# One ring and one order for all transfers of a scale-and-add kernel, with a head block of 512 rows

## The chip, the cores and the metric

The kernel runs on one core of one Trainium2 chip. Times are device microseconds (us) of one execution; a quoted time is the median of several executions. The profile gives the span from the first to the last instruction, which is about 1.3 us shorter than the time.

## The reference, cut to what matters

```python
B, S, D = 1024, 16, 512        # bfloat16
x, y  = normal * 0.05          # (B, S, D): 16384 rows of 1 KiB each
gamma = 1e-4 * normal * 0.05   # (D)
return x + gamma * y
```

Two tensors of 16.78 MB are read and one is written: 50.33 MB for hardly any arithmetic. Because gamma is so small, a result that pairs the wrong rows of y with x can still pass the correctness test; one that misplaces x cannot.

## The kernel before

Each of the 128 partitions owns 128 consecutive rows. y is multiplied by gamma in place on VectorE (DVE), then x is added in place, in four pieces of 53, 11, 53 and 11 rows. x has a buffer of 64 rows only, so its later loads wait until the first add has freed their place. SP (SyncE) issues the loads on its ring, ACT (ScalarE) issues gamma and the stores on its own. In the lists, `('x', 64, 117, 0)` is rows 64 to 117 of every partition, loaded to buffer row 0.

```python
PIECES = [53, 11, 53, 11]
SP = [('y', 0, 4), ('y', 4, 64), ('x', 0, 64, 0), ('y', 64, 128), ('x', 64, 117, 0), ('x', 117, 128, 64)]
ACT = [('g',), ('s', 0, 64), ('s', 64, 128)]
RELEASE = ('x', 64, 117, 0)
...
    xv = xf.rearrange("(p n) d -> p n d", p=P)       # 128 KiB from partition to partition
...
            if kind == "s" and not went:              # the first store waits for the hold
                _take(s_go, 1, eng)
                went = True
            if need > known:                          # and for the adds of its rows
                eng.wait_ge(s_add, need)
                known = need
...
    _take(s_load[RELEASE], 16, nc.tensor)             # x 64-117 has landed:
    nc.tensor.sem_inc(s_go, 1)                        # stores may be issued
    nc.tensor.sem_inc(s_rel, 1)                       # and VectorE may add
```

I call the last part *the hold*: no store is issued before x 64-117 has landed.

Of the kernel before, what the change touches and what calls it, by code (L numbers as in the profile page):

```python
# [3 lines left out]


PIECES = [53, 11, 53, 11]



SP = [('y', 0, 4), ('y', 4, 64), ('x', 0, 64, 0), ('y', 64, 128), ('x', 64, 117, 0), ('x', 117, 128, 64)]  # L10
ACT = [('g',), ('s', 0, 64), ('s', 64, 128)]

EARLY = (2, 0)


RELEASE = ('x', 64, 117, 0)

DVE = [('m', 0), ('m', 1), ('a', 0), ('a', 1), ('m', 2), ('m', 3), ('a', 2), ('a', 3)]
MULT, ADD = mybir.AluOpType.mult, mybir.AluOpType.add


def _take(sem, n, eng):


    return eng.wait_ge(sem, n).then_inc(sem, -n)  # L25


def kernel(
    tc: tile.TileContext,
    x: bass.AP,  # L30
    y: bass.AP,
    gamma: bass.AP,
    out: bass.AP,
):



    nc = tc.nc
    P = nc.NUM_PARTITIONS
    tc.close()  # L40
    tc.compile()  # L41

    xf = x.flatten_outer_dims()
    yf = y.flatten_outer_dims()
    of = out.flatten_outer_dims()
    N, D = xf.shape
    rows = N // P
    n = len(PIECES)
    assert sum(PIECES) == rows
    starts = [sum(PIECES[:c]) for c in range(n + 1)]  # L50
    dt = xf.dtype
    xv = xf.rearrange("(p n) d -> p n d", p=P)
    yv = yf.rearrange("(p n) d -> p n d", p=P)
    ov = of.rearrange("(p n) d -> p n d", p=P)

    gamma_row = nc.alloc_sbuf_tensor("gamma_row", [1, D], dt).ap()
    ones_row = nc.alloc_sbuf_tensor("ones_row", [1, P], dt).ap()
    gamma_sb = nc.alloc_sbuf_tensor("gamma_sb", [P, D], dt).ap()
    y_sb = nc.alloc_sbuf_tensor("y_sb", [P, rows, D], dt).ap()
    x_loads = [w for w in SP + ACT if w[0] == "x"]  # L60
    y_loads = [w for w in SP + ACT if w[0] == "y"]
    stores = [w for w in SP + ACT if w[0] == "s"]
    for loads in (x_loads, y_loads, stores):
        assert sum(w[2] - w[1] for w in loads) == rows
    x_rows = max(w[3] + w[2] - w[1] for w in x_loads)
    x_sb = nc.alloc_sbuf_tensor("x_sb", [P, x_rows, D], dt).ap()
    gamma_ps = nc.alloc_psum_tensor("gamma_ps", [P, D], mybir.dt.float32).ap()

    sem = nc.alloc_semaphore
    s_gamma, s_ones, s_ps, s_dve = sem("s_gamma"), sem("s_ones"), sem("s_ps"), sem("s_dve")  # L70
    s_load = {w: sem("s_" + "_".join(map(str, w[:2]))) for w in x_loads + y_loads}
    s_add, s_go, s_rel, s_end, s_out = sem("s_add"), sem("s_go"), sem("s_rel"), sem("s_end"), sem("s_out")
    added = [a for kind, *a in DVE if kind == "a"]
    order = {a[0]: k for k, a in enumerate(added)}

    def meets(a, b, c, d):
        return a < d and c < b

    def pieces_of(a, b):
        return [c for c in range(n) if meets(starts[c], starts[c + 1], a, b)]  # L80

    def x_at(row):
        return next(w[3] + row - w[1] for w in x_loads if w[1] <= row < w[2])

    def frees(w):

        c = set()
        for v in x_loads[: x_loads.index(w)]:
            lo, hi = max(v[3], w[3]), min(v[3] + v[2] - v[1], w[3] + w[2] - w[1])
            if lo < hi:  # L90
                c |= set(pieces_of(v[1] + lo - v[3], v[1] + hi - v[3]))
        return sorted(c)

    early = []

    def ring(eng, what, n_early):

        known, went = 0, False
        for k, w in enumerate(what):
            kind = w[0]  # L100
            need = frees(w) if kind == "x" else pieces_of(w[1], w[2]) + list(w[3:]) if kind == "s" else []
            need = max((order[c] + 1 for c in need), default=0)
            if kind == "s" and not went:
                _take(s_go, 1, eng)
                went = True
            if need > known:
                eng.wait_ge(s_add, need)
                known = need
            if kind == "g":
                i = eng.dma_start(out=gamma_row, in_=gamma.unsqueeze(0)).then_inc(s_gamma, 16)  # L110
            elif kind == "x":
                to = x_sb[:, w[3] : w[3] + w[2] - w[1], :]
                i = eng.dma_start(out=to, in_=xv[:, w[1] : w[2], :]).then_inc(s_load[w], 16)
            elif kind == "y":
                r = slice(w[1], w[2])
                i = eng.dma_start(out=y_sb[:, r, :], in_=yv[:, r, :]).then_inc(s_load[w], 16)
            else:
                r = slice(w[1], w[2])
                i = eng.dma_start(out=ov[:, r, :], in_=y_sb[:, r, :]).then_inc(s_out, 16)
            if k < n_early:  # L120
                early.append(i.ins)

    ring(nc.sync, SP, EARLY[0])
    ring(nc.scalar, ACT, EARLY[1])


    nc.vector.memset(ones_row, 1.0).then_inc(s_ones, 1)  # L127
    _take(s_ones, 1, nc.tensor)
    _take(s_gamma, 16, nc.tensor)
    nc.tensor.matmul(gamma_ps, ones_row, gamma_row, start=True, stop=True).then_inc(s_ps, 1)  # L130
    _take(s_ps, 1, nc.vector)
    nc.vector.tensor_copy(out=gamma_sb, in_=gamma_ps).then_inc(s_dve, 1)  # L132
    _take(s_dve, 1, nc.vector)

    _take(s_load[RELEASE], 16, nc.tensor)
    nc.tensor.sem_inc(s_go, 1)
    nc.tensor.sem_inc(s_rel, 1)

    landed, open_mults = set(), 0

    def need(loads, c):
        for w in loads:
            if w not in landed and meets(starts[c], starts[c + 1], w[1], w[2]):
                if w == RELEASE:
                    _take(s_rel, 1, nc.vector)
                else:
                    _take(s_load[w], 16, nc.vector)
                landed.add(w)

    for kind, *args in DVE:  # L150
        c = args[0]
        yt = y_sb[:, starts[c] : starts[c + 1], :]
        if kind == "m":
            need(y_loads, c)
            g = gamma_sb[:, None, :].to_broadcast([P, PIECES[c], D])
            nc.vector.tensor_tensor(out=yt, in0=yt, in1=g, op=MULT).then_inc(s_dve, 1)  # L156
            open_mults += 1
        else:
            need(x_loads, c)
            if open_mults:  # L160
                _take(s_dve, open_mults, nc.vector)
                open_mults = 0
            at = x_at(starts[c])
            xt = x_sb[:, at : at + PIECES[c], :]
            nc.vector.tensor_tensor(out=yt, in0=xt, in1=yt, op=ADD).then_inc(s_add, 1)  # L165


    nc.scalar.sem_inc(s_end, 1)
    _take(s_end, 1, nc.sync)
    _take(s_add, n, nc.sync)  # L170
    _take(s_out, 16 * len(stores), nc.sync)

    main = nc.main_func.blocks[0].instructions
    names = {i.name for i in early}
    for b in nc.main_func.blocks[1:]:
        for i in [i for i in b.instructions if i.name in names]:
            b.instructions.remove(i)
    for k, i in enumerate(early):
        main.insert(1 + k, i)
# [30 lines left out]
```

## Time and profile before

| | before |
|---|---|
| time, median of 3 | 119.98 us (119.96 to 120.91) |
| span of the profile | 118.7 us |
| VectorE busy | 70.0 us (59%) |
| packets of both rings, share of 16 engines' span | 66.0% + 32.6% |

The lines of the page, the issue list and the timeline are in the prediction. One view is added here, the waits of SP's own queue: who waited for whom, us in total, times, longest us.

```profile
SPq L25 <- SPq L25: 62.0, 2, 39.3
SPq L113 <- DVE y_sb L165: 53.0, 1, 53.0
```

The second line is SP standing still before it issues x 64-117, until the first add is done. It costs nothing: x 64-117 is issued from 55.78 on, and the transfers issued earlier keep the engines busy until y 64-128 lands at 60.56. The first is its two waits at the program's end.

Some numbers below come from the trace's records of single DMA packets and of completions, which no printed view lists: a packet's start, bytes and duration, and the time at which each of the 16 engines completed a transfer. I say "packet records" where I use them.

### The profile page before, as it was taken

How to read it: one execution, taken by the hardware profiler on the slowest of the kernel's cores; microseconds unless marked ns; L12 is line 12 of the kernel's file. 1: busy time of each engine (PE TensorE's matmuls, PEld its weight loads, DVE VectorE, ACT ScalarE, POOL GpSimd, SP SyncE). 2: the span in 40 equal slices, each digit the busy share in tenths (PEclk: the TensorE clock that was granted, in tenths of full speed). 3: DMA queues.
4: the chain of work that ended last, by engine and by line, in shares of the span. 5: the costliest groups of instructions: out<-in, count | busy, mean ns of one | idle time of the engine just before them, and what ended most of it. 6: DMA issues, size and time to landing. Idle time of an engine off the chain costs nothing. (4 is left out here: it accounts for less than half of the span.)

```text
span 118.7 us, 80 instructions
## 1 busy us (share of the span) xinstructions
PE 0.6 (0%) x1; PEld 0.1 (0%) x1; DVE 70.0 (59%) x10; POOL 0.2 (0%) x4
## 2 busy tenths in 40 slices
PE   0001000000000000000000000000000000000000
PEld 0000000000000000000000000000000000000000
DVE  0002000599999299999759999999999910000000
POOL 0000000000000000000000000000000000000000
DMA  8977977998899888998896969498899889988891
GB/s 268 571 332 331 663 331 331 596 464 353 353 486 574 353 353 353 640 420 353 353 585 293 585 293 585 205 634 353 353 596 464 353 353 420 640 353 353 353 663 44
DMA packets 1154, 50.33 MB, mean 424 GB/s; under 512 B 129, under 2 KB 130, under 8 KB 258
## 3 DMA queue, kind: packets, MB, share of 16 engines
q1 hardware_dynamic: 864, 33.55, 66.0%
q10 hardware_dynamic: 290, 16.78, 32.6%
HBM read 33.56 MB, written 16.78 MB: 424 GB/s over the span
## 5 line engine op out<-in xcount | busy, mean ns | idle before, releaser
L156 DVE TENSOR_TENSOR y_sb<-y_sb,gamma_sb 128x27136 bf16<-128x27136 bf16 (+1 forms) x4 | 34.6, 8688 | 12.3 <-DVEq L25 12.3
L165 DVE TENSOR_TENSOR y_sb<-x_sb,y_sb 128x27136 bf16<-128x27136 bf16 (+1 forms) x4 | 34.6, 8689 | 2.3 <-DVEq L25 2.2
L132 DVE CAST gamma_sb<-gamma_ps 128x512 bf16<-128x512 f32 x1 | 0.7, 692 | 8.8 <-DVEq L25 8.8
L127 DVE MEMSET ones_row<- 1x128 bf16 x1 | 0.2, 165 | 2.0 <-PEq L41 2.0
L130 PE MATMUL gamma_ps<-gamma_row,ones_row 1*128 1x512 bf16 x1 | 0.6, 577 | 10.2 <-PEq L25 10.2
L130 PEld LDWEIGHTS gamma_ps<-gamma_row,ones_row 1*128 1x128 bf16 x1 | 0.1, 99 | 10.2 <-issue 10.2
L194 POOL MEMSET const-bfloat16-1.0<- 128x1 bf16 x1 | 0.1, 101 | 0.0
L194 POOL MEMSET const-uint8-127<- 128x1 uint8 x1 | 0.1, 101 | 0.0
L194 POOL MEMSET const-float32-0.0<- 128x1 f32 x1 | 0.1, 98 | 0.2 <-issue 0.2
L194 POOL MEMSET const-float32-1.0<- 128x1 f32 x1 | 0.1, 98 | 0.0
## 6 DMA issues: line engine op xcount, KB each, us to landing
y_sb<-in_y_dram SPq DMA_DIRECT2D x1, 7680.0 KB, 21.4
x_sb<-in_x_dram SPq DMA_DIRECT2D x1, 6784.0 KB, 20.8
x_sb<-in_x_dram SPq DMA_DIRECT2D x1, 1408.0 KB, 23.8
y_sb<-in_y_dram SPq DMA_DIRECT2D x1, 512.0 KB, 3.8
out_dram<-y_sb ACTq DMA_DIRECT2D x2, 22.8
x_sb<-in_x_dram SPq DMA_DIRECT2D x1, 39.3
gamma_row<-in_gamma_dram ACTq DMA_DIRECT2D x1, 1.0 KB
y_sb<-in_y_dram SPq DMA_DIRECT2D x1, 58.3
```

The source lines that it names most:

```text
L127: nc.vector.memset(ones_row, 1.0).then_inc(s_ones, 1)
L130: nc.tensor.matmul(gamma_ps, ones_row, gamma_row, start=True, stop=True).then_inc(s_ps, 1)
L132: nc.vector.tensor_copy(out=gamma_sb, in_=gamma_ps).then_inc(s_dve, 1)
L156: nc.vector.tensor_tensor(out=yt, in0=yt, in1=g, op=MULT).then_inc(s_dve, 1)
L165: nc.vector.tensor_tensor(out=yt, in0=xt, in1=yt, op=ADD).then_inc(s_add, 1)
L194: nc = _bacc.Bacc("TRN2", target_bir_lowering=False, num_devices=1)
```

## The change

The intent: put every transfer on one ring in the order in which it is wanted, so that no hold and no second ring are needed; and let the first, small loads read one contiguous block.

```diff
-SP = [('y', 0, 4), ('y', 4, 64), ('x', 0, 64, 0), ('y', 64, 128), ('x', 64, 117, 0), ('x', 117, 128, 64)]
-ACT = [('g',), ('s', 0, 64), ('s', 64, 128)]
-RELEASE = ('x', 64, 117, 0)
+HEAD = 4
+RING = [("y", 0, HEAD), ("y", HEAD, 64), ("x", 0, HEAD, 0), ("x", HEAD, 64, HEAD), ("y", 64, 128),
+        ("x", 64, 117, 0), ("x", 117, 128, 64),
+        ("s", 0, HEAD), ("s", HEAD, 64), ("s", 64, 128)]
...
-    xv = xf.rearrange("(p n) d -> p n d", p=P)      # and yv, ov
+    def rows_of(t, a, b):
+        head = t[: P * HEAD].rearrange("(p n) d -> p n d", p=P)
+        body = t[P * HEAD :].rearrange("(p n) d -> p n d", p=P)
+        return head[:, a:b, :] if b <= HEAD else body[:, a - HEAD : b - HEAD, :]
...
-            if kind == "s" and not went:
-                _take(s_go, 1, eng)
-                went = True
...
-    _take(s_load[RELEASE], 16, nc.tensor)
-    nc.tensor.sem_inc(s_go, 1)
-    nc.tensor.sem_inc(s_rel, 1)
...
-    nc.scalar.sem_inc(s_end, 1)
-    _take(s_end, 1, nc.sync)
```

So three things change together: the layout (head block, and 124 rows and thus 124 KiB per partition for the rest), the ring of the stores, and the hold.

More of the change, by code (lines that the diff above doesn't have):

```diff
@@ L3 @@
 from concourse import mybir
+HEAD = 4
 PIECES = [53, 11, 53, 11]
-SP = [('y', 0, 4), ('y', 4, 64), ('x', 0, 64, 0), ('y', 64, 128), ('x', 64, 117, 0), ('x', 117, 128, 64)]
-ACT = [('g',), ('s', 0, 64), ('s', 64, 128)]
-EARLY = (2, 0)
-RELEASE = ('x', 64, 117, 0)
-DVE = [('m', 0), ('m', 1), ('a', 0), ('a', 1), ('m', 2), ('m', 3), ('a', 2), ('a', 3)]
+RING = [
+    ("y", 0, HEAD),
+    ("y", HEAD, 64),
+    ("x", 0, HEAD, 0),
+    ("x", HEAD, 64, HEAD),
+    ("y", 64, 128),
+    ("x", 64, 117, 0),
+    ("x", 117, 128, 64),
+    ("s", 0, HEAD),
+    ("s", HEAD, 64),
+    ("s", 64, 128),
+]
+EARLY = 2
+DVE = [("m", 0), ("m", 1), ("a", 0), ("a", 1), ("m", 2), ("m", 3), ("a", 2), ("a", 3)]
 MULT, ADD = mybir.AluOpType.mult, mybir.AluOpType.add
@@ L51 @@
     dt = xf.dtype
-    xv = xf.rearrange("(p n) d -> p n d", p=P)
-    yv = yf.rearrange("(p n) d -> p n d", p=P)
-    ov = of.rearrange("(p n) d -> p n d", p=P)
+    def rows_of(t, a, b):
+        head = t[: P * HEAD].rearrange("(p n) d -> p n d", p=P)
+        body = t[P * HEAD :].rearrange("(p n) d -> p n d", p=P)
+        return head[:, a:b, :] if b <= HEAD else body[:, a - HEAD : b - HEAD, :]
     gamma_row = nc.alloc_sbuf_tensor("gamma_row", [1, D], dt).ap()
@@ L59 @@
     y_sb = nc.alloc_sbuf_tensor("y_sb", [P, rows, D], dt).ap()
-    x_loads = [w for w in SP + ACT if w[0] == "x"]
-    y_loads = [w for w in SP + ACT if w[0] == "y"]
-    stores = [w for w in SP + ACT if w[0] == "s"]
-    for loads in (x_loads, y_loads, stores):
-        assert sum(w[2] - w[1] for w in loads) == rows
+    x_loads = [w for w in RING if w[0] == "x"]
+    y_loads = [w for w in RING if w[0] == "y"]
+    stores = [w for w in RING if w[0] == "s"]
+    for transfers in (x_loads, y_loads, stores):
+        assert sum(w[2] - w[1] for w in transfers) == rows
     x_rows = max(w[3] + w[2] - w[1] for w in x_loads)
@@ L71 @@
     s_load = {w: sem("s_" + "_".join(map(str, w[:2]))) for w in x_loads + y_loads}
-    s_add, s_go, s_rel, s_end, s_out = sem("s_add"), sem("s_go"), sem("s_rel"), sem("s_end"), sem("s_out")
-    added = [a for kind, *a in DVE if kind == "a"]
-    order = {a[0]: k for k, a in enumerate(added)}
+    s_add, s_out = sem("s_add"), sem("s_out")
+    added = [c for kind, c in DVE if kind == "a"]
+    order = {c: k for k, c in enumerate(added)}
     def meets(a, b, c, d):
@@ L94 @@
     early = []
-    def ring(eng, what, n_early):
-        known, went = 0, False
-        for k, w in enumerate(what):
-            kind = w[0]
-            need = frees(w) if kind == "x" else pieces_of(w[1], w[2]) + list(w[3:]) if kind == "s" else []
-            need = max((order[c] + 1 for c in need), default=0)
-            if kind == "s" and not went:
-                _take(s_go, 1, eng)
-                went = True
-            if need > known:
-                eng.wait_ge(s_add, need)
-                known = need
-            if kind == "g":
-                i = eng.dma_start(out=gamma_row, in_=gamma.unsqueeze(0)).then_inc(s_gamma, 16)
-            elif kind == "x":
-                to = x_sb[:, w[3] : w[3] + w[2] - w[1], :]
-                i = eng.dma_start(out=to, in_=xv[:, w[1] : w[2], :]).then_inc(s_load[w], 16)
-            elif kind == "y":
-                r = slice(w[1], w[2])
-                i = eng.dma_start(out=y_sb[:, r, :], in_=yv[:, r, :]).then_inc(s_load[w], 16)
-            else:
-                r = slice(w[1], w[2])
-                i = eng.dma_start(out=ov[:, r, :], in_=y_sb[:, r, :]).then_inc(s_out, 16)
-            if k < n_early:
-                early.append(i.ins)
-    ring(nc.sync, SP, EARLY[0])
-    ring(nc.scalar, ACT, EARLY[1])
+    known = 0
+    for k, w in enumerate(RING):
+        kind, r = w[0], slice(w[1], w[2])
+        need = frees(w) if kind == "x" else pieces_of(w[1], w[2]) if kind == "s" else []
+        need = max((order[c] + 1 for c in need), default=0)
+        if need > known:
+            nc.sync.wait_ge(s_add, need)
+            known = need
+        if kind == "x":
+            to = x_sb[:, w[3] : w[3] + w[2] - w[1], :]
+            i = nc.sync.dma_start(out=to, in_=rows_of(xf, w[1], w[2])).then_inc(s_load[w], 16)
+        elif kind == "y":
+            i = nc.sync.dma_start(out=y_sb[:, r, :], in_=rows_of(yf, w[1], w[2])).then_inc(s_load[w], 16)
+        else:
+            i = nc.sync.dma_start(out=rows_of(of, w[1], w[2]), in_=y_sb[:, r, :]).then_inc(s_out, 16)
+        if k < EARLY:
+            early.append(i.ins)
+    nc.scalar.dma_start(out=gamma_row, in_=gamma.unsqueeze(0)).then_inc(s_gamma, 16)
     nc.vector.memset(ones_row, 1.0).then_inc(s_ones, 1)
@@ L133 @@
     _take(s_dve, 1, nc.vector)
-    _take(s_load[RELEASE], 16, nc.tensor)
-    nc.tensor.sem_inc(s_go, 1)
-    nc.tensor.sem_inc(s_rel, 1)
     landed, open_mults = set(), 0
-    def need(loads, c):
-        for w in loads:
+    for kind, c in DVE:
+        for w in y_loads if kind == "m" else x_loads:
             if w not in landed and meets(starts[c], starts[c + 1], w[1], w[2]):
-                if w == RELEASE:
-                    _take(s_rel, 1, nc.vector)
-                else:
-                    _take(s_load[w], 16, nc.vector)
+                _take(s_load[w], 16, nc.vector)
                 landed.add(w)
-    for kind, *args in DVE:
-        c = args[0]
         yt = y_sb[:, starts[c] : starts[c + 1], :]
         if kind == "m":
-            need(y_loads, c)
             g = gamma_sb[:, None, :].to_broadcast([P, PIECES[c], D])
@@ L158 @@
         else:
-            need(x_loads, c)
             if open_mults:
```

## The prediction

The sum came to about -0.2 us (0 + 0 + 0.08 - 0.25 + 0), from 119.98 to 119.8. Of its terms, the 0.08 was an allowance per packet and per completion; the 0.0 for the pitch stands as the estimate; the -0.25 is the choice of a part of the measured 0.67.

> **What bounds the kernel now.** I read four things in this order: the page's busy shares, the DMA rows of the page, the list of transfers with their times from issue to landing, and the timeline. The question for each is whether the engine, or only the 16 DMA engines, could be what sets the end. First the page:
>
> ```profile
> span 118.7 us, 80 instructions
> PE 0.6 (0%) x1; PEld 0.1 (0%) x1; DVE 70.0 (59%) x10; POOL 0.2 (0%) x4
> ...
> DMA  8977977998899888998896969498899889988891
> ...
> DMA packets 1154, 50.33 MB, mean 424 GB/s; under 512 B 129, under 2 KB 130, under 8 KB 258
> ...
> q1 hardware_dynamic: 864, 33.55, 66.0%
> q10 hardware_dynamic: 290, 16.78, 32.6%
> ```
>
> The reader is to see that VectorE works 59% of the span, while the two rings' packets together take 66.0 + 32.6 = 98.6% of all that 16 engines have. The tenths in the DMA row look lower than that because a long packet is counted coarsely there; the ring shares are sums of packet times. So the kernel is bound by transfers, and the end can only come earlier if bytes go, if the rate rises, or if the 1.4% of unused engine time (1.7 us) shrinks.
>
> Next, the DMA issues and the timeline, cut to what carries the order:
>
> ```profile
> y_sb<-in_y_dram SPq DMA_DIRECT2D x1, 7680.0 KB, 21.4
> x_sb<-in_x_dram SPq DMA_DIRECT2D x1, 6784.0 KB, 20.8
> x_sb<-in_x_dram SPq DMA_DIRECT2D x1, 1408.0 KB, 23.8
> y_sb<-in_y_dram SPq DMA_DIRECT2D x1, 512.0 KB, 3.8
> out_dram<-y_sb ACTq DMA_DIRECT2D x2, 22.8
> x_sb<-in_x_dram SPq DMA_DIRECT2D x1, 39.3
> ```
>
> ```profile
> 0.00 0.84 SPq L116 DMA_DIRECT2D y_sb<-in_y_dram  x2
> ...
> 1.90 0.33 SPq L113 DMA_DIRECT2D x_sb<-in_x_dram  x1
> ...
> 2.28 0.51 SPq L116 DMA_DIRECT2D y_sb<-in_y_dram  x1
> ...
> 41.46 17.29 DVE L165 TENSOR_TENSOR y_sb<-x_sb,y_sb 128x27136 bf16<-128x27136 bf16 x2 [2.17 <-DVEq L25]
> 55.78 0.81 SPq L113 DMA_DIRECT2D x_sb<-in_x_dram  x2
> 60.69 17.29 DVE L156 TENSOR_TENSOR y_sb<-y_sb,gamma_sb 128x27136 bf16<-128x27136 bf16 x2 [1.94 <-DVEq L25]
> 76.95 18.85 ACTq L119 DMA_DIRECT2D out_dram<-y_sb  x2
> 78.13 17.30 DVE L165 TENSOR_TENSOR y_sb<-x_sb,y_sb 128x27136 bf16<-128x27136 bf16 x2
> ```
>
> The last number of an issue row is us from issue to landing; in the timeline the first number is the start. Adding them gives when each load was complete (two digits from the trace's completion records): y rows 0-4 at 3.76, y 4-64 at 21.86, x 0-64 at 41.21, y 64-128 at 60.56, x 64-117 at 76.60, x 117-128 at 79.99; the stores at 99.36 and 118.67. The differences are the engines' work on each:
> y 4-64: 7.864 MB in 18.10 us, 434.5 GB/s; x 0-64 and y 64-128: 8.389 MB in 19.35 us each, 433.5; x 64-117: 6.947 MB in 16.04, 433; x 117-128: 1.442 MB in 3.39, 425; both stores: 16.777 MB in 38.68, 433.7.
> Sum 114.91 us for 49.81 MB: one constant rate, loads and stores alike. Ahead of it lie 3.76 us for the first half megabyte, behind it 0.03 us. Packet by packet the trace says the same: from 1.2 us to 117 us there is no microsecond in which the 16 engines together idle even 15 ns.
>
> [...]
>
> **The change part by part.**
> Stores from ACT's ring to SP's. Removed: the wait that held the stores until x 64-117 had landed (TensorE passed that signal on) and one small wait at the end. On SP's single ring the stores stand behind all loads anyway. Before, the first store was issued at 76.95, and its packets began at 79.06, the moment the first engine had finished x 117-128: no gap there to close. Value 0.0 us.
>
> One store ring, three stores. The order on SP is y 0-4, y 4-64, x 0-4, x 4-64, y 64-128, x 64-117, x 117-128, and stores 0-4, 4-64, 64-128. Two waits on VectorE still stand in it. x 64-117 waits for the first add, done at 41.46 + 14.29 (the mean of the 27136-column form) = 55.75, while the engines are busy until 60.56: 4.8 us to spare. Stores 0-4 and 4-64 can be issued directly after, by about 59 us. The last store waits for the last add: VectorE starts at 60.69 on y 64-128 and does 4 instructions, 2 x 14.29 + 2 x 3.08 = 34.74, so 95.43. The engines are busy with the preceding store until about 98.4 for the first engine (79.06 + 8 packets x 2.418). From issue to first packet takes 1.0 us (first y transfer, 0.00 to 1.00). So it comes about 1.9 us before it is needed: no gap. Value 0.0 us.
>
> More and smaller packets. x 0-4 and store 0-4 are 128 packets of 4 KiB each, 8 per engine. Such a packet took 155 ns from start to start; one of 60 KiB 2263; together 2418, and the 64 KiB packet that they replace 2418. So splitting costs nothing visible[...].
>
> Issue time. SP issues one load more while y 4-64 is under way, 0.3 to 0.5 us, with over 18 us of queued work in front of it: hidden. gamma stays on ACT; the first multiply needs y 4-64 at 21.86, gamma was ready at 11.7: hidden.
>
> The first 512 rows as a block. This is the only part that touches engine time that is really lost. In the packet records the first packets of 4 KiB take 198 to 1155 ns; the mean of all 128 is 239 against 155 in the steady part. (239 - 155) x 8 = 0.67 us per engine are lost at the start. Before, these packets read places 128 KiB apart; now they read one contiguous 512 KiB. If all of this loss comes from the spread, 0.67 us go. But [...]the next load now begins in places nobody has touched before (before, it continued right after the first rows). I choose a third to a half: -0.25 us.
>
> 124 KiB pitch of the rest: same packet sizes,[...] 0.0[...].
>
> Sum: 0 + 0 + 0.08 - 0.25 + 0 = about -0.2 us, from 119.98 to **119.8 us**.
>
> **The rivals.**
> First, the start could improve fully, -0.67 us[...]. For it: the first packets are uneven, 198 to 1155 ns. Against it: later loads that begin in fresh places (x at 21 us) show no packet above 2446 beside a mean of 2421, so fresh places cost almost nothing once the engines are running[...].
> Second, the single ring could stop: a transfer at its head waits for VectorE and everything behind it with it. The last store is the candidate, because its add ends only 3 us before the engines run dry. If VectorE came 3 us later, the gap would be about 1 us and the time 121. Against it: VectorE's four instructions start with the landing of y 64-128 and have fixed lengths, so add and engines shift together.
> Third, 64 KiB packets that start at multiples of 4 KiB rather than 64 KiB, at the 124 KiB pitch, could meet worse in HBM. One per cent less rate would be 1.16 us: 121.1. Nothing in the profile speaks for it, nothing excludes it; the 60 KiB packets of y, which start off a 64 KiB boundary, ran at 434.5, which speaks against.
> Fourth, loads and stores could overlap and slow each other, which the removed wait may have been there to avoid. In one ring each engine passes from load to store once, as before, with the 0.6 us of stagger between engines that the completions show (118.06 to 118.67): no change.
>
> **Range and chances.** [...]losses that I can name are 1 us each and unlikely. The three runs before lie at 119.96, 119.98 and 120.91, so a median may move by some tenths on its own. Eight times in ten I expect 119.2 to 120.5. A change of 2% is 2.4 us[...]: faster 0.02, within 2% 0.96, slower 0.02.
>
> **What would show it right or wrong.** Right: all packets on SP's ring but gamma's, ring share still about 98 to 99%, stores landing 38.7 us after the last load, VectorE's eight instructions with the same lengths, and y 0-4 landing a few tenths before 3.76 with every later landing earlier by the same amount. Wrong: a stretch without packets between the second and the last store (second rival), a 64 KiB packet that takes clearly more or less than 2420 ns (third, or a pitch effect that I denied), or a first landing unchanged or later, which would make the contiguous block worthless.

## The result, and the profile after

The changed kernel takes 121.21 us (120.78 to 121.68, 6 runs), the kernel before 119.97 (119.83 to 120.91, 6 runs). The ratio is 1.0102, 95% interval 1.0072 to 1.0133. At a threshold of 2% this is "the same", but it is clearly 1% slower, and it lies above the predicted range.

The page after, beside the page lines in the prediction:

```profile
span 120.1 us, 77 instructions
PE 0.6 (0%) x1; PEld 0.1 (0%) x1; DVE 70.0 (58%) x10; POOL 0.2 (0%) x4
...
DMA packets 1443, 50.33 MB, mean 419 GB/s; under 512 B 162, under 2 KB 163, under 8 KB 547
...
q1 hardware_dynamic: 1440, 50.33, 98.1%
```

VectorE does exactly what it did, 70.0 us. The bytes are the same 50.33 MB, all on one ring. The engines are about as full as before, 98.1% for 98.6%, in a span that is 1.4 us longer. So the time did not go into a gap: the same bytes took longer to move. (The busy share does not show that. From 76 to 80 us it is 0.98 here and 0.98 in after_held, a kernel of the experiments, at 339 and 413 GB/s.)

The issue rows (us from issue to landing) and the timeline of the same kernel say where:

```profile
x_sb<-in_x_dram SPq DMA_DIRECT2D x1, 6784.0 KB, 20.8
x_sb<-in_x_dram SPq DMA_DIRECT2D x1, 1408.0 KB, 24.9
y_sb<-in_y_dram SPq DMA_DIRECT2D x1, 512.0 KB, 3.2
```

```profile
56.12 0.81 SPq L117 DMA_DIRECT2D x_sb<-in_x_dram  x2
56.98 39.20 SPq L121 DMA_DIRECT2D out_dram<-y_sb  x3
61.08 17.29 DVE L144 TENSOR_TENSOR y_sb<-y_sb,gamma_sb 128x27136 bf16<-128x27136 bf16 x2 [1.99 <-DVEq L34]
```

The first y transfer lands after 3.2 us instead of 3.8: the contiguous block does start quicker. x 64-117 takes 20.8 as before. The last load, x 117-128, takes 24.9 instead of 23.8: over a microsecond appears within 1.4 MB. And the stores are now issued from 56.98, while before the first was issued at 76.95.

Landing by landing, last of 16 engines (completion records):

| landed, us | before | after | difference |
|---|---|---|---|
| y 0-4 | 3.76 | 3.21 | -0.55 |
| y 4-64 | 21.86 | 21.88 | +0.02 |
| x up to 64 | 41.21 | 41.56 | +0.35 |
| y 64-128 | 60.56 | 60.95 | +0.39 |
| x 64-117 | 76.60 | 76.94 | +0.34 |
| x 117-128 | 79.99 | 81.36 | +1.37 |
| last store | 118.67 | 120.10 | +1.43 |

In the last engine the quick start is gone again at the second landing. In the mean of the 16 engines, from the same records, 0.47 us of it become 0.16 there and nothing at y 64-128 (60.32 after, 60.28 before); the +0.34 to +0.39 us in the table are one engine, which is 0.26 us behind the second last at y 4-64 and 0.51 at x up to 64. The last load loses 1.0 us. The stores themselves lose nothing more. In the packet records the 11 KiB packets of x 117-128 take 512 ns on average (up to 1091) where they took 424 before; that is 8 x 0.088 = 0.7 us per engine. The rest is one engine: after, the last of the 16 completions comes 0.75 us behind the second last (120.10 and 119.35), before 0.07 us (118.67 and 118.60).

The waits of SP's queue after:

```profile
SPq L117 <- DVE y_sb L152: 52.8, 1, 52.8
SPq L121 <- DVE y_sb L152: 38.0, 2, 36.4
```

SP now also waits, on line 121, for the adds before it issues stores, 36.4 us of it for the last one. That wait ended in time: the last store came at 56.98 + 39.20 = 96.18 less its own 0.3 us of issuing (0.33 for one load in the timeline before), and the previous store landed only at 100.79.

### The profile page after: what moved, and what is told of

It reads as the page before. It is cut to its first block, busy times and chain, and to the rows that moved or that the text cites. A ratio compares the mean times of both kernels' runs of the same rounds, so it can differ in the third digit from the quotient of the medians.

```text
span 120.1 us, 77 instructions
## 1 busy us (share of the span) xinstructions
PE 0.6 (0%) x1; PEld 0.1 (0%) x1; DVE 70.0 (58%) x10; POOL 0.2 (0%) x4
## 2 busy tenths in 40 slices
DMA packets 1443, 50.33 MB, mean 419 GB/s; under 512 B 162, under 2 KB 163, under 8 KB 547
## 3 DMA queue, kind: packets, MB, share of 16 engines
q1 hardware_dynamic: 1440, 50.33, 98.1%
## 6 DMA issues: line engine op xcount, KB each, us to landing
x_sb<-in_x_dram SPq DMA_DIRECT2D x1, 6784.0 KB, 20.8
x_sb<-in_x_dram SPq DMA_DIRECT2D x1, 1408.0 KB, 24.9
```

## The experiments

There are two losses to explain, the slow last load and the late engine, and two suspects, the layout and the ring. Eighteen runs were made, three of them repeats (after_again, layout_again, store_old_again). Edits are against the changed kernel unless said otherwise. "Two rings" means the kernel before with its list split at row 4, so that the new layout can be used there. Several kernels read or write wrong rows; it is said each time.

### Which part: after_again, ring_only, layout_only, x_old

after_again is the changed kernel, unchanged.

> The changed kernel once more, to see what repeats in a second profile. Theory A (the new layout makes reads slower; the 11 KiB packets of x 117-128 suffer most): about 121.2 us, the 11 KiB packets again 80 to 100 ns above 422 on average (0.6 to 0.8 us per engine), one engine 0.4 to 0.7 us behind the others at the end. Theory B (stores queued behind the last load on one ring disturb it): the same here. Theory C (an accident of that one profile): the slow stretch at 77 to 79 us is absent and the time is near 120.5.

Measured: 121.06 us (120.70 to 121.27), ratio 1.0079 (1.0060 to 1.0098). The 11 KiB packets took 491 ns, the late engine was 0.55 us behind. Both losses repeat.

ring_only keeps the ring of ten transfers and takes the old layout:

```diff
-        head = t[: P * HEAD].rearrange("(p n) d -> p n d", p=P)
-        body = t[P * HEAD :].rearrange("(p n) d -> p n d", p=P)
-        return head[:, a:b, :] if b <= HEAD else body[:, a - HEAD : b - HEAD, :]
+        return t.rearrange("(p n) d -> p n d", p=P)[:, a:b, :]
```

> One ring and the same list of ten transfers, but every partition owns 128 consecutive rows as before; right result. Theory A: 119.9 to 120.1 us, 11 KiB packets at 422 ns, first y packets again slow at the start (240 ns on average). Theory B: 0.6 to 0.8 us above before, 11 KiB packets still slow.

Measured: 120.76 us, ratio 1.0056 (1.0038 to 1.0074). The 11 KiB packets took 501 ns; the late engine was only 0.13 us behind. Theory A falls: the slow last load belongs to the ring, not to the layout.

layout_only is the opposite, an edit of the kernel before:

```diff
-SP = [('y', 0, 4), ('y', 4, 64), ('x', 0, 64, 0), ...
-ACT = [('g',), ('s', 0, 64), ('s', 64, 128)]
+SP = [('y', 0, 4), ('y', 4, 64), ('x', 0, 4, 0), ('x', 4, 64, 4), ...
+ACT = [('g',), ('s', 0, 4), ('s', 4, 64), ('s', 64, 128)]
...
-in_=xv[:, w[1] : w[2], :]
+in_=rows_of(xf, w[1], w[2])          # y and out likewise
```

> The new layout with the two rings of before (stores on ACT, held until x 64-117 landed); right result. Theory A: 121.0 to 121.4 us, the whole loss, with slow 11 KiB packets. Theory B: 120.2 to 120.5 (only the scattered slower reads), 11 KiB packets at 422 ns.

Measured: 120.43 us (120.03 to 120.80), ratio 1.0029 (1.0010 to 1.0048). The 11 KiB packets took 422 ns, every one; the late engine was 0.51 us behind. So the two losses are separate: the ring brings the slow last load, 0.56%, the layout the late engine, 0.29%. Together 0.85%, and the changed kernel measured 0.79% on the same chip.

x_old reads x in the old layout inside the changed kernel (a wrong result):

```diff
+        if t is xf:
+            return t.rearrange("(p n) d -> p n d", p=P)[:, a:b, :]
         head = t[: P * HEAD].rearrange("(p n) d -> p n d", p=P)
```

> The changed kernel, but x is read in the old layout, so each partition adds rows of x that do not belong to its rows of y: a wrong result on purpose. Theory A: the slow 11 KiB packets go, 0.6 to 0.8 us are won, about 120.5; y's packets stay slightly long. Theory B: nothing changes, 121.2.

Measured: 120.88 us, ratio 1.0067; 11 KiB packets at 523 ns although they now read at the old addresses; the late engine gone (0.03 us). Theory A misses again. What went, in this profile, is the late engine, and between the medians 0.18 us of time (121.06 to 120.88). The profile is of the fastest of the six runs (120.65), and the lag differs from profile to profile (0.41 to 0.86 us where there is one), so one profile and six runs need not agree.

### Why the ring: ring_held, ring_plain, held_mult

Two things distinguish stores on the single ring: they share it with the loads, and they are issued some 20 us earlier, because the hold is gone. ring_held gives ring_only its hold back:

```diff
+        if kind == "s" and w[1] == 0:
+            _take(s_go, 1, nc.sync)
...
+    release = next(w for w in x_loads if w[1] == 64)
+    _take(s_load[release], 16, nc.tensor)
+    nc.tensor.sem_inc(s_go, 1)
+    nc.tensor.sem_inc(s_rel, 1)
```

> The single ring with the old layout, ten transfers, but the stores are issued only when x 64-117 has landed, as the kernel before does (same signal through TensorE); right result. Theory B1 (it hurts that stores stand in the ring from 57 us on, while the last load is still coming): 120.0 to 120.2 us, 11 KiB packets at 422 ns. Theory B2 (it hurts that loads and stores share a ring, whenever they are issued): 120.6 to 120.9, still 60 to 100 ns too long.

Measured: 120.06 us, ratio 0.9999 (0.9984 to 1.0013). The whole loss is gone, with all transfers still on one ring. The view of one stretch, 76 to 80 us, shows it. The columns are the stretch, its length, busy us of PE, PEld, DVE and POOL, the granted clock, the DMA engines' busy share and GB/s. First ring_only, then ring_held:

```profile
76.00:80.00 4.00, 0.00 (x0) 0.00 (x0) 3.85 (x2) 0.00 (x0) 1.00 0.97 345
```

```profile
76.00:80.00 4.00, 0.00 (x0) 0.00 (x0) 3.85 (x2) 0.00 (x0) 1.00 0.98 409
```

VectorE works the same 3.85 us in both, and the engines count as busy in both; but they move 345 GB/s instead of 409. Read the last column, not the share before it. (The two kernels have the same packets there. The same row of the kernel before, whose 64 KiB store packets start in the stretch, reads 1.38 and 592 GB/s and cannot be compared with these.)

ring_plain asks whether the 4 KiB store packets right behind the load matter, by going back to the eight transfers of before:

```diff
-    ("x", 0, HEAD, 0),
-    ("x", HEAD, 64, HEAD),
+    ("x", 0, 64, 0),
...
-    ("s", 0, HEAD),
-    ("s", HEAD, 64),
+    ("s", 0, 64),
```

(against ring_only)

> The single ring with the old layout and the eight transfers of before: x 0-64 in one, stores 0-64 and 64-128, issued without a hold; right result. Theory B3 (the 4 KiB store packets right behind the last load hurt): 120.0 to 120.2 us. B1 and B2: 120.6 to 120.9, as the ring with ten transfers, because the first store packet of 64 KiB stands in the same place.

Measured: 120.82 us, ratio 1.0068; 11 KiB packets at 513 ns. No: 64 KiB store packets do the same, and the two extra transfers cost nothing (120.82 with eight, 120.76 with ten).

held_mult moves the hold 1.7 us earlier, in ring_only, with a small fill on VectorE behind the multiply of piece 2 as the signal.

```diff
+        if kind == "s" and w[1] == 0:
+            _take(s_go, 1, nc.sync)
...
             open_mults += 1
+            if c == 2:
+                nc.vector.memset(mark, 1.0).then_inc(s_go, 1)
```

> Single ring, old layout, ten transfers; SP issues the stores when the multiply of piece 2 is done, about 75 us (a small VectorE fill behind it gives the signal); right result. If what counts is that stores stand behind the last load's packets when these are read, from about 76 us: 120.6 to 120.9 and slow 11 KiB packets. If the long stay in the ring from 57 us counts: 120.0 to 120.2.

Measured: 120.64 us, ratio 1.0056 (1.0037 to 1.0075); 11 KiB packets at 510 ns. The issue times in the timelines bracket it, ring_held first, held_mult second:

```profile
77.02 18.84 SPq L122 DMA_DIRECT2D out_dram<-y_sb  x3
```

```profile
75.36 20.65 SPq L123 DMA_DIRECT2D out_dram<-y_sb  x3
```

Issued at 77.02 the stores cost nothing, at 75.36 as much as at 57. So in these runs it isn't the long stay in the ring that matters, but whether the stores are there when the engines come to the end of the last load: undisturbed, its packets end near 79.6 (79.62 in ring_held), and the lengthened ones begin at 76.5 here and at 77.1 in ring_only.

### Does it need short packets: even_tail, swap_loads

even_tail gives the last two x loads 32 rows each, 32 KiB packets:

```diff
-PIECES = [53, 11, 53, 11]
+PIECES = [53, 11, 32, 32]
...
-    ("x", 64, 117, 0),
-    ("x", 117, 128, 64),
+    ("x", 64, 96, 0),
+    ("x", 96, 128, 32),
```

(against ring_plain)

> Single ring, old layout, eight transfers, no hold; the last two x loads are 32 rows each (and the last two VectorE pieces too), so the load ahead of the stores consists of 32 KiB packets instead of 11 KiB; right result. If stores behind a load cost a fixed 0.6 to 0.75 us per engine at the turn: 120.6 to 120.9 us, the last loads' packets in sum 0.6 to 0.75 us too long. If short packets are needed for the loss: 120.0 to 120.2 and 32 KiB packets at one constant length.

Measured: 120.89 us, ratio 1.0067 (1.0054 to 1.0079). The last two packets of each engine, those that start after 76.6 us, took 1406 to 2067 ns, all others about 1213; in sum 0.93 us per engine.

swap_loads, against ring_plain, loads the 53 KiB packets last:

```diff
-    ("x", 64, 117, 0),
     ("x", 117, 128, 64),
+    ("x", 64, 117, 0),
```

> Single ring, old layout, eight transfers, no hold; x 117-128 is loaded ahead of x 64-117, so 53 KiB packets stand ahead of the stores; right result. VectorE gets x 64-117 at 80.0 instead of 76.6, its last add ends near 97.5 instead of 95.4 and the last store may come some tenths late. If the loss needs short packets: 11 KiB and 53 KiB packets at 422 and 2004 ns, time 120.0 to 120.6 from the late add alone. If the turn costs the same for any packet: the last 53 KiB packets 0.6 to 0.75 us too long in sum, 120.7 to 121.3.

Measured: 120.76 us, ratio 1.0060 (1.0047 to 1.0073). The 11 KiB packets, now with a load behind them, took 428 ns. The very last 53 KiB packet of each engine took 2613 to 3182 ns instead of 2004; in sum 0.94 us per engine. In these runs the loss came at the turn from loads to stores with every packet size tried (11, 32 and 53 KiB), and only in the last 3 to 4 us before it.

### What the hold was worth on two rings: two_rings_unheld

The kernel before with only the hold taken away:

```diff
-            if kind == "s" and not went:
-                _take(s_go, 1, eng)
-                went = True
...
-    _take(s_load[RELEASE], 16, nc.tensor)
-    nc.tensor.sem_inc(s_go, 1)
-    nc.tensor.sem_inc(s_rel, 1)
```

> The kernel before with only the hold taken away: stores on ACT's ring, waiting for their adds alone; right result. If an engine alternates between rings by packet, the first store (ready at 59 us) shares the engines with x 64-117, which lands near 95 instead of 76.6, the last add ends near 113, and the time is 132 to 136 us. If the rings do not share like that: 120 to 121.

Measured: 133.87 us, ratio 1.1155. The timeline:

```profile
55.62 0.81 SPq L110 DMA_DIRECT2D x_sb<-in_x_dram  x2
58.62 53.75 ACTq L116 DMA_DIRECT2D out_dram<-y_sb  x2
60.54 17.29 DVE L147 TENSOR_TENSOR y_sb<-y_sb,gamma_sb 128x27136 bf16<-128x27136 bf16 x2 [1.96 <-DVEq L25]
94.71 17.30 DVE L156 TENSOR_TENSOR y_sb<-x_sb,y_sb 128x27136 bf16<-128x27136 bf16 x2 [16.87 <-DVEq L25]
```

VectorE's last adds start at 94.71 instead of 78.13, with 16.87 us of idleness before them, because the first store shares the engines with x 64-117. The engines then have nothing to do until the last add ends at 112, as the zeros in this kernel's GB/s row show:

```profile
GB/s 454 296 555 333 463 426 316 632 316 493 454 316 632 316 316 632 316 381 458 316 577 262 545 348 577 262 561 332 350 400 0 0 0 79 553 316 632 316 316 316
```

So the hold had two jobs. On two rings it kept the stores from delaying a load that VectorE needs; without it, this run took about 14 us more. The single ring does that job by its order (ring_plain, also without a hold: 120.82 us). The second job, keeping stores away from the load ahead of them, 0.7 us, the order does not do.

The packet records of this run show that the second loss is not tied to the single ring. On each engine the one load packet just ahead of its first store packet, which starts from 64.66, took 2773 to 3093 ns instead of 2004, 0.97 us too long on average. After that, 53 KiB loads and 64 KiB stores alternate one by one until about 90 us, and the loads keep 2004 ns and the stores about 2420. The loss was paid once per engine, at the first meeting.

### Where the late engine comes from: head_only, pitch_only, store_old, y_head_spread, store_new and repeats

All of these are edits of layout_only: two rings with the hold. head_only reads the contiguous first rows but everything else at 128 KiB (wrong rows):

```diff
-        return head[:, a:b, :] if b <= HEAD else body[:, a - HEAD : b - HEAD, :]
+        return head[:, a:b, :] if b <= HEAD and t is not of else whole[:, a:b, :]
```

> Two rings and hold of before; x and y read their first 512 rows as a contiguous block, everything else at 128 KiB from partition to partition; the store is as before, so rows do not match: a wrong result on purpose. If the block's quicker start is worth its 0.3 to 0.5 us by itself: 119.6 us, y 0-4 landing at 3.2 to 3.4 and y 4-64 at 21.4 to 21.6. If the first memory delay is only moved to the next packets: 119.9 to 120.1 and y 4-64 at 21.8 to 21.9.

Measured: 119.92 us, ratio 0.9992 (0.9979 to 1.0004). y 0-4 landed at 3.38, y 4-64 at 21.61. Between the two expectations: of a start 0.38 us quicker 0.25 are left at the second landing and 0.06 at the end (span 118.6).

pitch_only reads the first rows spread as before and the rest at 124 KiB (wrong result):

```diff
-        return head[:, a:b, :] if b <= HEAD else body[:, a - HEAD : b - HEAD, :]
+        return whole[:, a:b, :] if b <= HEAD or t is of else body[:, a - HEAD : b - HEAD, :]
```

> Two rings and hold of before; the first four rows of a partition are read 128 KiB apart as before, the rest at 124 KiB; the store as before: a wrong result on purpose. If the 124 KiB pitch costs the layout's loss: 120.4 to 120.8 us, y 0-4 at 3.76, many load packets 20 to 150 ns long, one engine late. If pitch is innocent: 120.0.

Measured: 119.97 us, ratio 0.9993 (0.9978 to 1.0007), no late engine (0.03 us). The pitch by itself is innocent.

store_old has all loads in the new layout and the stores in the old (wrong result), y_head_spread the whole new layout but for y's first four rows (wrong rows of y, within the test's tolerance):

```diff
+        if t is of:                       # store_old
+        if t is yf and b <= HEAD:         # y_head_spread
+            return t.rearrange("(p n) d -> p n d", p=P)[:, a:b, :]
```

> Two rings and hold; loads wholly in the new layout (contiguous first rows and 124 KiB pitch), stores in the old: a wrong result on purpose. Theory L1 (the loads' combination of contiguous first rows and new pitch costs): 120.3 to 120.5. Theory L2 (the stores' new layout costs): 119.9 to 120.0, store packets at 2418 and 2267 here and longer with the new layout.

> Two rings and hold; the new layout except that y's first four rows are read 128 KiB apart as before: a wrong result on purpose. Theory L1a (after a contiguous first load the 16 engines run in step, within 0.2 us, and then meet at the 124 KiB pitch): with the spread start they are 0.5 us apart again and the time is 119.9 to 120.1. Otherwise 120.3 to 120.5.

Measured: store_old 120.06 us, ratio 1.0006 (0.9988 to 1.0024), late engine 0.19 us. y_head_spread 120.13 us (119.92 to 120.86), ratio 1.0019 (0.9976 to 1.0063), unclear in time, but one engine late by 0.41 us in its profile, from the first load on. So engines running in step after a contiguous first load do not explain it.

The pair was repeated in a later session, with store_new beside it, the opposite of store_old (`if t is not of`; wrong result).

> The whole new layout on two rings with the hold, once more: 120.2 to 120.6 us with runs up to 0.8 us apart, and one engine 0.3 to 0.6 us behind the others, if the layout's loss is real; 119.9 to 120.1 if it was an accident of that chip.

> Loads in the new layout, stores in the old, once more (wrong result on purpose). Theory L2 (the stores' layout costs): 119.9 to 120.15 again, runs within 0.2 us. Theory L1 (the loads' layout costs): 120.2 to 120.6 like the whole layout beside it.

> Loads in the old layout, stores in the new (wrong result on purpose), two rings with the hold. Theory L2: 120.2 to 120.6, although the store packets keep 2267 and 2418 ns. Theory L1: 119.9 to 120.1, runs within 0.2 us.

Measured: layout_again 120.40 us (119.96 to 120.75), ratio 1.0024 (1.0006 to 1.0042), one engine 0.86 us late (the profile is of its slowest run). store_old_again 120.15 us, ratio 1.0009 (0.9996 to 1.0022), 0.13 us. store_new 119.98 us, ratio 1.0000 (0.9985 to 1.0015), 0.01 us. The layout's loss is real: it came back in a second session with an interval above 1. The stores' layout alone does not bring it: L2 falls. L1 is not borne out either, as new loads with old stores lost about a third of it in the mean (1.0006 and 1.0009), with intervals that include no loss at all.

### The remedy: after_held

The changed kernel with the hold, as in ring_held.

> The changed kernel with one thing put back: SP issues the stores only when x 64-117 has landed; right result. Theory: what the early issue of the stores costs (0.68 us) goes, what the layout costs on two rings (0.35 us) stays: 120.3 to 120.5 us, 11 KiB packets at 422 ns. If the layout costs nothing on one ring: 120.0.

Measured: 120.24 us (119.97 to 120.77), ratio 1.0030 (0.9984 to 1.0076); 11 KiB packets at 422 ns; late engine 0.42 us. In the stretch from 76 to 80 us the changed kernel, first, and this one, second:

```profile
76.00:80.00 4.00, 0.00 (x0) 0.00 (x0) 3.85 (x2) 0.00 (x0) 1.00 0.98 339
```

```profile
76.00:80.00 4.00, 0.00 (x0) 0.00 (x0) 3.85 (x2) 0.00 (x0) 1.00 0.98 413
```

The ring's loss is gone, and the layout's late engine is still there. What it costs here is not resolved: the medians differ by 0.17 us, and the interval includes no loss. No version tried beat the kernel before: ring_held equals it, and the kernels whose median came out a little below it, head_only, pitch_only and store_new, give wrong results and lie within 0.1%.

Over all profiles, packet records at the turn and the lag of the last engine sort the kernels cleanly. The loss at the turn is (mean packet minus undisturbed packet) times packets per engine; the lag is the last of the final completions less the second last.

| | stores issued from | loss at the turn, us | lag of one engine, us | ratio |
|---|---|---|---|---|
| before | 76.95, ACT | 0.01 | 0.07 | 1 |
| changed; again | 57, SP | 0.72; 0.55 | 0.75; 0.55 | 1.0102; 1.0079 |
| ring_only | 57, SP | 0.63 | 0.13 | 1.0056 |
| ring_held | 77.02, SP | 0.06 | 0.05 | 0.9999 |
| held_mult | 75.36, SP | 0.70 | 0.15 | 1.0056 |
| layout_only; again | 77, ACT | 0.00; 0.02 | 0.51; 0.86 | 1.0029; 1.0024 |
| after_held | 77.05, SP | 0.00 | 0.42 | 1.0030 |

One engine late by 0.4 us or more is found in the profiles with the new layout for body and stores of all three tensors (changed, again, layout_only, again, after_held, y_head_spread), and in no other, where the lag is 0.19 us at most. The mean of the 16 final completions shows the two losses apart: 118.34 us before, 118.26 to 118.44 in layout_only, layout_again and after_held, but 119.01 to 119.12 in the changed kernel, its repeat, ring_only and held_mult. In these profiles the unheld ring slows all engines, and the layout slows one.

## Why the prediction was wrong

**What bounds the kernel.** Right: transfers, with VectorE beside them. VectorE's instructions kept their lengths, and its last add came in time.

**"Stores from ACT's ring to SP's ... Value 0.0 us."** This is the step that failed. I took the removed hold for a mere ordering device, which the ring's order replaces. It also kept the stores out of the ring until the last load was nearly through. Without it ring_only lost 0.56%, about 0.7 us; with it back on the same ring, ring_held lost nothing. The fourth rival named the right object, "which the removed wait may have been there to avoid", and dismissed it because each engine passes from load to store once, as before. It does, but the passage itself cost 0.55 to 0.94 us per engine when the stores already stood behind the loads, and at most 0.06 us when they were issued in the last 2.6 us of the load (ring_held: 77.02, its packets ending near 79.6). My gap analysis could not have found this: I looked for engines without work, and the loss is in engines with work.

**"The first 512 rows as a block ... -0.25 us."** Wrong at the end, right at the start. y 0-4 landed 0.55 us earlier, more than I allowed, but the first 60 KiB packet of each engine then took 2327 to 2661 ns instead of 2267. All of y 4-64 together lost 0.34 us per engine, and at the second landing the last engine had nothing left. The prediction named the risk, and weighed it too lightly, but the reason it gave, places that nobody has touched before, does not hold: in pitch_only y 4-64 begins in such places too, after spread first rows, and there these packets took 2267 to 2289 ns. In all nine profiles whose first y rows are contiguous y 4-64 lost 0.16 to 0.34 us per engine, in the eleven with spread ones 0.08 at most. So the start's loss is largely moved to the next load; why is open. The block with the old pitch for the rest (head_only) kept 0.06 us of it in its span.

**"124 KiB pitch of the rest ... 0.0."** Right for the pitch alone (0.9993). Whole, the layout cost 0.24 to 0.29% through one late engine, which no rival of mine contained. Why an engine falls behind is not settled. Neither the head, the pitch, the stores' layout, nor new loads with old stores showed it by itself.

**"More and smaller packets."** Right that splitting costs nothing visible: 120.82 us with eight transfers, 120.76 with ten.

**The other rivals.** The single ring did not stop for VectorE: there was no stretch without packets before the last store. The third, worse addresses for 64 KiB packets, is not what happened: the stores kept 2418 ns. The loads of y 64-128 did get longer, 2435 ns on average for 2422, 0.10 us per engine.

**Two readings of the profile.** That the engines never idle from 1.2 us on is not quite so: from 1.3 to 1.8 us only 14 of the 16 had a packet in progress. And gamma's late landing (10.11), which a passage took as a sign of rings alternating by packet, does not show that: its packet ran at 7.47, after two 60 KiB packets of its engine. The alternation is seen in two_rings_unheld, where 53 KiB loads and 64 KiB stores took turns until about 90 us. Neither changed the forecast.

**The sum.** I had 0 + 0.08 - 0.25 = -0.2 us, the 0.08 an allowance that no trace shows. The runs give, for ring, packets and layout, about 0.7 + 0 + 0.3 = 1.0 us, and the changed kernel measured 0.95 (0.79% of 120.05) in those rounds, 1.2 in the first. The chances for "within 2%" were right; the range, 119.2 to 120.5, was not.

What stays open besides the late engine is the mechanism at the turn: no trace here shows it. Measured are the bracket, the full loss with stores issued at 75.36 and 0.06 us with 77.02, and the single loss per engine in two_rings_unheld, where the first store was issued at 58.62, its packets started from 64.66, after two load packets per engine, and the later loads, with stores between them, kept 2004 ns.

## What to carry to other kernels

In a kernel bound by transfers, look at the length of packets of one size, not only for gaps: here a busy share of 98.1% hid a stretch at 339 GB/s, where the held ring moved 413. Before a wait is removed as redundant, ask for every thing it delays; here a hold that looked like ordering also kept stores out of the ring at the turn from loads to stores. In a kernel like this one, try issuing the first store only when the last load but one has landed; on the single ring in the old layout that took 120.06 us, and 120.76 without it.
